# High parts of weight sums one step later, and blocks decoded one quad later, in an attention and two-layer kernel

## Chip, cores and metric

One core of a Trainium2 chip. The metric is the device time of one execution in microseconds (us), as the median of several runs.

## What is computed

```python
def reference(**kwargs):
    attn_out = _attn_ref(**attn_kwargs)        # chunked linear attention with decay, (4, 8, 768, 32)
    x = attn_out.transpose(0, 2, 1, 3).reshape(B * S, H * D)          # 3072 tokens x 256
    x = _moe_ref(x=x, **moe_kwargs)            # h = max(x @ w_in, 0);  (h * h) @ w_out
    return _moe2_ref(x=x, **moe2_kwargs)       # h = x @ w_in; (h * clip(h + 3, 0, 6) / 6) @ w_out
```

Both layers have 256 inputs and outputs and 2048 inner columns; all values are float32.

## The kernel before

**Tiles.** The 3072 tokens make six tiles of 512 columns, 0 to 5. The inner columns make 16 blocks of 128, or eight pairs of them, `q`. Every float32 operand is held as two numbers, a high part (ScalarE's rounding to the matmul's type) and a low part (the remainder, by VectorE or GpSimd), and each product is three matmuls: high by high, low by high, high by low.

**Stages.** Attention and the first layer of tiles 0 to 3 run together in 64 steps, numbered 0 to 63 (`ORDER`); a step is one tile and one inner block, with six matmuls into `h` (L582) and six into `y` (L616). After the matmuls of a step, ScalarE writes `ga` (the relu), VectorE squares it (L595; in some early steps ScalarE), ScalarE makes its high part `gha` (L597), and VectorE its low part `gla` (L599); the `y` matmuls of a step come two steps later. Steps 48 to 63 are tile 3; `ga3_5` is tile 3, inner block 5, step 53.

From there on the tiles are worked in pairs, by 32 *quads*, numbered 0 to 31: quads 0 to 7 are the first layer of tiles 4 and 5 (`a`), quads 8 to 15, 16 to 23 and 24 to 31 the second layer of three pairs of tiles (`b`, 0 to 2). A quad is one `q`: two inner blocks by two tiles. Its four products into the inner layer are made with seven, by sums and differences of the operands: weight sums in slots 0 to 10 of a block (4 to 6 are the sums that a product needs beside the weights), and operands `b11`, `b21`, `b22`, `t1` to `t4`, each with sum, high and low. Products are named p1 to p7, and collect in three PSUM banks, X, V and Z (L732): X p1, V p2, X p6, X p7, Z p5, X p4, Z p3. ScalarE copies X out as `s1`, `u2` and `u3` (L737) before the next product adds to it, and VectorE adds (L741) to get the four results `c11`, `c22`, `c12`, `c21`; c22 is taken from Z before p3 adds to Z. Then come the nonlinearity (L749 to L766), high parts `ghc` (L772), low parts `glc` (L775), and six matmuls into `y` for each (L788).

**Weight blocks.** The first layer's weights are already split for steps 0 to 63. For its quads the sums are needed too: `Weights.renew(q)` adds high and low (`whole`, VectorE, L507) and makes four sums (`sums`, GpSimd, L500); `Weights.both(q)` then makes high parts (`high`, ScalarE, L537: tiles `ea`, three slots, and `ah`, one slot) and low parts (`lower`, GpSimd, L544). The second layer's blocks `j` (0 to 15, two for each `q`) come from memory as they are decoded: `early` (E, ScalarE, L477), `begin` (B, VectorE, two operations `lowb`, L481 and L486), `end` (M: VectorE's merge into `wtb`, L491; GpSimd's sums for even `j`; the load of block `j` + 2), then high and low of the first slots and of the sums (F, G: `part`) or of all (H: `both`).

**What sets the order.** The schedule is written out by hand: each engine runs what is emitted, in that order, and waits by semaphores. `at(g, point, f)` hangs a job on a place: `g` below 64 is a step, where the jobs run after `gha` is issued and before `gla`; 1000 + g is quad g with points 0, 1, 6, 2, 3, 5, 4 in the order of `emit`. For the second layer's blocks a table of strings, one for each quad, gives point, letter and block: `5M10` is `end(10)` at point 5. For the operands, rows give the distance in quads from the first quad that uses them, the point, `s`, `h`, `l` or `L` (sum, high, low by VectorE, low by GpSimd), and the operand:

```python
    for q in range(NQ - 2):
        at(52 + 2 * q, 0, lambda q=q: w1.renew(q))
        at(53 + 2 * q, 0, lambda q=q: w1.both(2 * q))
```

Here NQ is 8: blocks 0 to 5 take steps 52 to 63, blocks 6 and 7 quads 0 and 1.

Of the kernel before, what the change touches and what calls it, by code (L numbers as in the profile page):

```python
# [41 lines left out]
NQ = DFF // (2 * P)  # L42
# [36 lines left out]
def attn_mlp_mlp(ctx: ExitStack, tc, a, bT, cT, bK, x, w1i, w1o, w2i, w2o, yT):  # L79
# [352 lines left out]
    class Weights:  # L432
# [21 lines left out]
        def at(self, q, k, i, n=1):  # L454

            if (self.pre, q) in own:
                return own[self.pre, q][k][:, i:i + n]
            if 4 <= i < 7:
                return self.ext[q][:, i - 4 + 3 * (k == "l"):][:, 0:n]
            d = self.hi if k == "h" else self.lo  # L460
            return d[q][:, i - 3 * (i > 6):][:, 0:n]
# [432 lines left out]
    w1 = w["a"] = Weights(w1i, w1o, "a")  # L894
# [122 lines left out]


    for q in range(NQ - 2):
        at(52 + 2 * q, 0, lambda q=q: w1.renew(q))  # L1020
        at(53 + 2 * q, 0, lambda q=q: w1.both(2 * q))
    for q in range(NQ - 2, NQ):
        at(1000 + q - 6, 5, lambda q=q: w1.renew(q))
        at(1001 + q - 6, 1, lambda q=q: w1.both(2 * q))
# [8 lines left out]
             "G": lambda j: w2.part(j, 1)}  # L1033
    for g, plan in enumerate(("6E2 2B2 5M2", "2E3 2B3 5M3", "2E4 2B4 5M4", "1F2 1G2 6H3 2E5 2B5 5M5",
# [3 lines left out]
        for d in plan.split():  # L1038
            at(1000 + g, int(d[0]), lambda f=does2[d[1]], j=int(d[2:]): f(j))
# [9 lines left out]
    def operands(g, key, plan):  # L1049
        for dg, p, f, n in plan:  # L1050
            if f == "s" and key == ("b", NPAIR - 1):
                at(g + dg, p, lambda n=n: later(key, n))
                continue
            at(g + dg, p, lambda f={"s": oper_sum, "h": oper_high, "l": oper_low, "L": by_pool}[f], n=n: f(key, n))
# [6 lines left out]
    operands(1000 + NQ, ("b", 0),  # L1061
# [4 lines left out]
    for p in range(1, NPAIR):  # L1066
        operands(1000 + NQ * (p + 1), ("b", p),
# [4 lines left out]

    def ready_second(t, f):
        run(16 * t + f, 1)
# [53 lines left out]
```

## Time and profile before

| | |
|---|---|
| median of 3 runs | 575.94 us (575.22 to 578.52) |
| profiled execution | 578.32 us, span of its instructions 576.5 us |
| mean granted TensorE clock | 0.988 of full speed |
| TensorE busy | 554.5 us, 96% of the span, 4110 matmuls |
| VectorE busy | 434.8 us, 75%, 669 instructions |
| ScalarE busy | 382.7 us, 66%, 692 instructions |
| GpSimd busy | 194.2 us, 34%, 260 instructions |
| chain that ended last, by engine | TensorE 85%, VectorE 7%, issue 3%, ScalarE 2%, GpSimd 2%, DMA 1% |

PE is TensorE, DVE VectorE, ACT ScalarE, POOL GpSimd. Times in the profile count from the start of the span. Line numbers (L537) are those of the kernel before; buffer numbers are left out of tile names, so `ea` in a row stands for `ea0` to `ea7`, and the number in a name such as `wta3s` is the block. The chain follows the last instruction back, at each step to what released it; "issue" is time in which an engine waited for nothing that the profile shows. An engine that waits for nothing starts its next instruction before the one ahead is shown as ended, so starts are nearer to each other than durations say.

### The profile page before, as it was taken

The page shows a single profiled execution, that of the slowest core. Times are in us where ns is not written, and L with a number is a line of the kernel's source. Part 1 is how long each engine was busy: PE and PEld are TensorE (multiplying, and loading weights), DVE is VectorE, ACT ScalarE, POOL GpSimd, SP SyncE. Part 2 cuts the span into 40 slices and gives each one's busy share as a digit, 9 for nine tenths or more (in the row PEclk, how much of TensorE's full clock was granted, in tenths as well). Part 3 has the DMA queues.
Part 4 walks back from the last instruction along what each step waited for, and adds up shares of the span by engine and source line. Part 5 has one row for each costly group of instructions (what it writes and reads, how often), then busy time and mean ns, then how long its engine had stood idle before and what let it go on. Part 6 is the DMA issues. An engine that isn't in the chain of part 4 may idle for free.

```text
span 576.5 us, 10490 instructions
## 1 busy us (share of the span) xinstructions
PE 554.5 (96%) x4110; PEld 442.3 (77%) x4110; DVE 434.8 (75%) x669; ACT 382.7 (66%) x692; POOL 194.2 (34%) x260
## 2 busy tenths in 40 slices
PE   7689999999999999799998999999999999999996
PEld 4457777778787877588886788888888888888884
DVE  8687777666555766698899998998967788776774
ACT  5576877455444655677787777787766678676663
POOL 3464443320000877476876632740000600000000
PEclk9789999999999999899999999999999999999999
DMA  7895453213000100111221111000200000200002
GB/s 209 204 253 158 121 148 111 74 49 101 2 1 26 49 0 2 35 40 36 74 74 36 55 56 38 0 2 0 74 0 1 1 2 1 74 0 1 0 2 73
DMA packets 26481, 31.43 MB, mean 55 GB/s; under 512 B 2144, under 2 KB 21056, under 8 KB 26432
## 3 DMA queue, kind: packets, MB, share of 16 engines
q1 hardware_dynamic: 24528, 29.85, 18.4%
q10 hardware_dynamic: 1904, 0.92, 0.6%
q8 instruction: 32, 0.52, 0.4%
q14 instruction: 17, 0.14, 0.1%
HBM read 27.41 MB, written 3.35 MB: 53 GB/s over the span
## 4 chain that ended last, share of the span: by engine, by line
PE 85%; DVE 7%; issue 3%; ACT 2%; POOL 2%; DMA 1%; SPq 0%; ACTq 0%; DVEq 0%; POOLq 0%
PE y L788 27%; PE ya L616 14%; PE X L732 14%; PE ha L582 14%; PE Z L732 7%; PE V L732 3%; PE att L363 2%; DVE glc L775 2%; DVE c L741 1%; PE att L350 1%; PE att L331 1%; PE big L890 1%; DVE c L764 1%; DMA xb<-in_x 1%; PE att L377 1%
## 5 line engine op out<-in xcount | busy, mean ns | idle before, releaser
L775 DVE TENSOR_TENSOR glc<-c,ghc 128x512 fp32r<-128x512 f32 x128 | 96.4, 759 | 8.1 <-ACT ghc L772 7.1
L772 ACT ACTIVATE ghc<-c 128x512 fp32r<-128x512 f32 x128 | 77.7, 629 | 2.4 <-DVE c L766 1.9
L788 PE MATMUL y<-glc,bh 128*128 128x512 f32 x192 | 74.9, 390 | 0.0
L788 PE MATMUL y<-ghc,bh 128*128 128x512 f32 x192 | 74.8, 390 | 0.0
L788 PE MATMUL y<-ghc,bl 128*128 128x512 f32 x192 | 74.7, 389 | 0.0
L766 DVE SCALAR_TENSOR_TENSOR c<-rc,c 128x512 f32<-128x512 f32 x72 | 52.7, 731 | 22.0 <-ACT rc L752 22.0
L752 ACT ACTIVATE rc<-c,three 128x512 f32<-128x512 f32 x72 | 52.0, 722 | 25.0 <-DVE c L741 24.9
L599 DVE TENSOR_TENSOR gla<-ga,gha 128x512 fp32r<-128x512 f32 x64 | 48.9, 764 | 24.1 <-ACT gha L597 23.3
L597 ACT ACTIVATE gha<-ga 128x512 fp32r<-128x512 f32 x64 | 40.6, 635 | 36.0 <-DVE ga L595 35.7
L595 DVE TENSOR_TENSOR ga<-ga,ha 128x512 f32<-128x512 f32 x48 | 32.9, 686 | 38.9 <-ACT ga L589 38.8
L741 DVE TENSOR_TENSOR c<-Z,u 128x512 f32<-128x512 f32 x64 | 43.9, 686 | 21.0 <-PE Z L732 20.4
L589 ACT ACTIVATE ga<-ha 128x512 f32<-128x512 f32 x64 | 37.8, 590 | 30.9 <-PE ha L582 30.9
L737 ACT COPY u<-X 128x512 f32<-128x512 f32 x64 | 37.6, 587 | 27.4 <-PE X L732 27.1
L616 PE MATMUL ya<-gha,ah 128*128 128x512 f32 x128 | 53.0, 414 | 0.2
L582 PE MATMUL ha<-act_h,ah 128*128 128x512 f32 x128 | 51.1, 401 | 2.3 <-ACT ah L522 2.3
L582 PE MATMUL ha<-act_h,al 128*128 128x512 f32 x128 | 51.1, 401 | 0.3 <-POOL al L524 0.2
L616 PE MATMUL ya<-gla,ah 128*128 128x512 f32 x128 | 50.7, 396 | 0.0
L616 PE MATMUL ya<-gha,al 128*128 128x512 f32 x128 | 50.7, 396 | 0.0
L582 PE MATMUL ha<-act_l,ah 128*128 128x512 f32 x128 | 50.6, 397 | 0.0
L544 POOL TENSOR_TENSOR bl<-wtb,bh 128x256 fp32r<-128x256 f32 (+1 forms) x34 | 30.5, 922 | 35.8 <-ACT bh L537 29.3
L788 PEld LDWEIGHTS y<-glc,bh 128*128 128x128 f32 x192 | 36.0, 188 | 8.4 <-DVE glc L775 0.9
L788 PEld LDWEIGHTS y<-ghc,bh 128*128 128x128 f32 x192 | 36.0, 188 | 7.7 <-ACT ghc L772 0.4
(295 smaller groups left out, 1247.1 us busy)
## 6 DMA issues: line engine op xcount, KB each, us to landing
rawa<-in_w1i SPq DMA_DIRECT2D x8, 512.0 KB
rawa<-in_w1o SPq DMA_DIRECT2D x8, 512.0 KB
rawb<-in_w2i SPq DMA_DIRECT2D x8, 512.0 KB
rawb<-in_w2o SPq DMA_DIRECT2D x8, 512.0 KB
xb<-in_x SPq DMA_DIRECT2D x24, 128.0 KB
ef<-scr SPq DMA_DIRECT2D x10, 256.0 KB
out_yT<-xf SPq DMA_DIRECT2D x10, 256.0 KB
bc<-in_cT SPq DMA_DIRECT2D x6, 256.0 KB
```

What stands on the lines that cost most here:

```text
L582: nc.tensor.matmul(out=h, lhsT=wt[fb][:, k, fo * P:fo * P + P], rhs=xt[t][:, k, :], start=i == 0, stop=i == 5)
L589: nc.scalar.activation(out=g, in_=h, func=AF.Relu)
L597: nc.scalar.activation(out=gh, in_=g, func=AF.Copy)
L599: nc.vector.tensor_tensor(out=gl, in0=g, in1=gh.bitcast(F32), op=ALU.subtract)
L616: nc.tensor.matmul(out=ys[m], lhsT=terms[i][0][fb][:, fo, m * P:m * P + P], rhs=terms[i][1], start=first and i == 0, stop=last and i == 2)
L732: nc.tensor.matmul(out=self.ps[bank], lhsT=lhsT, rhs=rhs, start=start and i == 0, stop=stop and i == 2, skip_group_check=True)
L741: nc.vector.tensor_tensor(out=self.sb[c], in0=self.ps[bank], in1=self.sb[n], op=ALU.add)
L752: nc.scalar.activation(out=self.sb["r" + c], in_=src, func=AF.Relu, bias=three)
L766: nc.vector.scalar_tensor_tensor(out=self.sb[c], in0=self.sb["r" + c], scalar=6.0, in1=src, op0=ALU.min, op1=ALU.mult)
L772: nc.scalar.activation(out=self.gh[c], in_=self.sb[c], func=AF.Copy)
L775: nc.vector.tensor_tensor(out=self.gl[c], in0=self.sb[c], in1=self.gh[c].bitcast(F32), op=ALU.subtract)
L788: nc.tensor.matmul(out=ys[t][m], rhs=terms[i][1], lhsT=w[self.pre].at(self.q, terms[i][0], 7 + 2 * (1 - f) + m)[:, 0], start=first and i = ...
```

## The change

Three things move. The high and low parts of blocks 0 to 4 of the first layer (`both`) go from one step after their sums to two, ahead of the next block's `renew`; those of block 5 go from step 63 to point 1 of quad 0. In the table of the second layer's blocks, block 10's B and M go to later points of quad 7, and all that concerned blocks 11 to 15 goes one quad later, F10 and G10 staying in quad 8. And in the operands' rows a few highs and lows move: the low of t3 of the first pair from point 5 to point 2 of quad 7; for the later pairs the highs of b11, b21 and t2 by a point or a few, and for pair 1 the low of t2 goes from VectorE to GpSimd.

```diff
--- before.py
+++ after.py
@@ -1017,8 +1017,10 @@
 
 
     for q in range(NQ - 2):
+        if q:
+            at(52 + 2 * q, 0, lambda q=q: w1.both(2 * q - 2))
         at(52 + 2 * q, 0, lambda q=q: w1.renew(q))
-        at(53 + 2 * q, 0, lambda q=q: w1.both(2 * q))
+    at(1000, 1, lambda: w1.both(2 * (NQ - 3)))
     for q in range(NQ - 2, NQ):
         at(1000 + q - 6, 5, lambda q=q: w1.renew(q))
         at(1001 + q - 6, 1, lambda q=q: w1.both(2 * q))
@@ -1033,7 +1035,7 @@
              "G": lambda j: w2.part(j, 1)}
     for g, plan in enumerate(("6E2 2B2 5M2", "2E3 2B3 5M3", "2E4 2B4 5M4", "1F2 1G2 6H3 2E5 2B5 5M5",
                               "1F4 1G4 6H5 2E6 2B6 5M6", "1E7 1B7 2M7 2E8 6F6 5B8 5M8 4G6", "1H7 6E9 2B9 2F8 5M9 4G8",
-                              "1H9 6E10 2B10 5M10", "6E11 2B11 2F10 5M11 5G10", "6E12 2B12 2H11 5M12",
+                              "1H9 6E10 5B10 4M10", "2F10 5G10", "6E11 2B11 5M11", "2H11 6E12 2B12 5M12",
                               "6E13 2B13 2F12 5M13 5G12", "6E14 2B14 2H13 5M14", "6E15 2B15 2F14 5M15 5G14", "2H15")):
         for d in plan.split():
             at(1000 + g, int(d[0]), lambda f=does2[d[1]], j=int(d[2:]): f(j))
@@ -1061,14 +1063,14 @@
     operands(1000 + NQ, ("b", 0),
              ((-4, 0, "s", "t1"), (-4, 2, "s", "t2"), (-4, 4, "h", "b11"), (-3, 1, "h", "b21"), (-3, 2, "s", "t4"),
               (-2, 0, "s", "t3"), (-2, 1, "h", "t2"), (-2, 1, "l", "b11"), (-2, 5, "l", "b21"), (-1, 1, "l", "t2"),
-              (-1, 1, "h", "t3"), (-1, 2, "h", "t1"), (-1, 2, "L", "t1"), (-1, 5, "l", "t3"), (-1, 4, "h", "t4"),
+              (-1, 1, "h", "t3"), (-1, 2, "h", "t1"), (-1, 2, "l", "t3"), (-1, 2, "L", "t1"), (-1, 4, "h", "t4"),
               (-1, 4, "L", "t4"), (0, 1, "h", "b22"), (0, 1, "L", "b22")))
     for p in range(1, NPAIR):
         operands(1000 + NQ * (p + 1), ("b", p),
-                 ((-4, 0, "s", "t1"), (-4, 2, "s", "t2"), (-3, 0, "s", "t4"), (-3, 2, "s", "t3"), (-3, 6, "h", "b11"),
-                  (-3, 5, "h", "b21"), (-2, 1, "l", "b11"), (-2, 6, "h", "t2"), (-2, 2, "l", "b21"), (-2, 5, "l", "t2"),
-                  (-1, 1, "h", "t3"), (-1, 2, "l", "t3"), (-1, 6, "h", "t1"), (-1, 5, "l", "t1"), (-1, 2, "h", "t4"),
-                  (0, 1, "l", "t4"), (-1, 5, "h", "b22"), (0, 2, "l", "b22")))
+                 ((-4, 0, "s", "t1"), (-4, 2, "s", "t2"), (-3, 0, "s", "t4"), (-3, 2, "s", "t3"), (-3, 1, "h", "b11"),
+                  (-2, 6, "h", "b21"), (-2, 1, "l", "b11"), (-2, 5, "h", "t2"), (-2, 2, "l", "b21"),
+                  (-2, 5, "L" if p == 1 else "l", "t2"), (-1, 1, "h", "t3"), (-1, 2, "l", "t3"), (-1, 6, "h", "t1"),
+                  (-1, 5, "l", "t1"), (-1, 2, "h", "t4"), (0, 1, "l", "t4"), (-1, 5, "h", "b22"), (0, 2, "l", "b22")))
 
     def ready_second(t, f):
         run(16 * t + f, 1)
```

ScalarE, steps 53 to 56, before (each name ends in a number of its own; `oa2b21` is an operand's high part):

```order
L597 ACTIVATE gha3_5_2745<-ga3_5_2747 128x512
L537 ACTIVATE ea0_2729<-wta0s_2728 128x384
L537 ACTIVATE ah0_342<-wta0s_2728 128x128
L589 ACTIVATE ga3_6_2773<-ha3_6_2764 128x512
L597 ACTIVATE gha3_6_2771<-ga3_6_2773 128x512
L685 ACTIVATE oa2b21_2790<-xin4_1965 128x512
L589 ACTIVATE ga3_7_2802<-ha3_7_2793 128x512
L597 ACTIVATE gha3_7_2800<-ga3_7_2802 128x512
L537 ACTIVATE ea1_2784<-wta1s_2783 128x384
L537 ACTIVATE ah1_430<-wta1s_2783 128x128
```

and now:

```order
L597 ACTIVATE gha3_5_2745<-ga3_5_2747 128x512
L589 ACTIVATE ga3_6_2768<-ha3_6_2759 128x512
L597 ACTIVATE gha3_6_2766<-ga3_6_2768 128x512
L537 ACTIVATE ea0_2729<-wta0s_2728 128x384
L537 ACTIVATE ah0_342<-wta0s_2728 128x128
L685 ACTIVATE oa2b21_2790<-xin4_1965 128x512
L589 ACTIVATE ga3_7_2802<-ha3_7_2793 128x512
L597 ACTIVATE gha3_7_2800<-ga3_7_2802 128x512
L589 ACTIVATE ga3_8_2823<-ha3_8_2814 128x512
L597 ACTIVATE gha3_8_2821<-ga3_8_2823 128x512
L537 ACTIVATE ea1_2784<-wta1s_2783 128x384
L537 ACTIVATE ah1_430<-wta1s_2783 128x128
```

`ea0` and `ah0` stand behind the `gha` of step 54 instead of step 53, and `ea1`, `ah1` behind that of step 56; blocks 2 to 4 likewise. On VectorE and GpSimd no row of these steps moves.

ScalarE, the end of step 63 and the start of quad 0, before:

```order
L597 ACTIVATE gha3_15_3020<-ga3_15_3022 128x512
L537 ACTIVATE ea5_3004<-wta5s_3003 128x384
L537 ACTIVATE ah5_1146<-wta5s_3003 128x128
L737 COPY s10_3043<-X0_3039 128x512
L685 ACTIVATE oa2b22_3058<-xin5_2366 128x512
L737 COPY u20_3063<-X0_3039 128x512
L772 ACTIVATE ghc11_0_3065<-c11_0_3049 128x512
```

and now:

```order
L597 ACTIVATE gha3_15_3020<-ga3_15_3022 128x512
L737 COPY s10_3038<-X0_3034 128x512
L537 ACTIVATE ea5_3004<-wta5s_3003 128x384
L537 ACTIVATE ah5_1146<-wta5s_3003 128x128
L685 ACTIVATE oa2b22_3058<-xin5_2366 128x512
L737 COPY u20_3063<-X0_3034 128x512
L772 ACTIVATE ghc11_0_3065<-c11_0_3044 128x512
```

The copy `s1` of quad 0 (printed `s10`, block X0) now stands ahead of `ea5` and `ah5`; the high of b22, `u2` and the rest stay behind them.

VectorE in quad 8, from the copy of the first layer's last output, before (`lowb` is the decoding, the row into `wtb` the merge):

```order
L800 COPY xf4_3935<-y0_01_3127 128x512
L481 TENSOR_SCALAR lowb11_3946<-rawb11_3754 128x512
L486 TENSOR_SCALAR lowb11_3946<-rawb11_3754 128x512
L741 TENSOR_TENSOR c22_8_3959<-Z8_3955,u38_3944 128x512
L800 COPY xf5_3964<-y0_11_3151 128x512
L766 SCALAR_TENSOR_TENSOR c22_8_3959<-rc22_8_3973,c22_8_3959 128x512
L491 SCALAR_TENSOR_TENSOR wtb5_3820<-wtb5_3820,lowb11_3946 128x512
L741 TENSOR_TENSOR c12_8_3987<-Z8_3955,u28_3924 128x512
```

and now:

```order
L800 COPY xf4_3934<-y0_01_3127 128x512
L741 TENSOR_TENSOR c22_8_3955<-Z8_3951,u38_3943 128x512
L800 COPY xf5_3960<-y0_11_3151 128x512
L766 SCALAR_TENSOR_TENSOR c22_8_3955<-rc22_8_3969,c22_8_3955 128x512
L741 TENSOR_TENSOR c12_8_3980<-Z8_3951,u28_3924 128x512
L775 TENSOR_TENSOR glc22_8_3983<-c22_8_3955,ghc22_8_3982 128x512
```

The decoding and the merge of block 11 are gone from this quad, and the addition for c22 follows the copy. In quad 7 the low of t3 now stands ahead of the addition of c22, the decoding of block 10 behind it, and its merge behind the low of c22.

## Rows read from the trace of the kernel before

**Rows 1.** Busy time of four stretches: us of length, then per engine busy us (instructions).
```profile
212.00:244.90 32.90, 29.66 (x112) 21.05 (x111) 21.63 (x33) 19.71 (x40) 20.40 (x33) 0.95 0.05 15
238.00:242.00 4.00, 3.97 (x11) 3.13 (x12) 3.35 (x6) 2.67 (x6) 0.89 (x3) 0.57 0.01 2
...
303.50:336.50 33.00, 30.05 (x128) 23.30 (x128) 31.41 (x43) 24.44 (x46) 20.58 (x23) 1.00 0.16 48
336.50:565.00 228.50, 228.50 (x1009) 189.03 (x1008) 180.63 (x277) 163.12 (x275) 34.18 (x42) 1.00 0.05 15
```

**Rows 2.** Chain of waits, 212 to 240: start us, us, what.
```profile
222.57 0.98 POOL wta3s L500
223.56 0.07 issue
...
224.46 0.02 ACT ea L537
```

**Rows 3.** Timeline of ScalarE: start us, us, instruction, [idle before <-releaser].
```profile
206.01 0.53 ACT L537 ACTIVATE ea<-wta0s 128x384 fp32r<-128x384 f32 x1 [2.24 <-POOL wta0s L500]
...
220.27 0.63 ACT L597 ACTIVATE gha<-ga 128x512 fp32r<-128x512 f32 x1 [0.76 <-DVE ga L595]
...
236.74 0.52 ACT L537 ACTIVATE ea<-wta5s 128x384 fp32r<-128x384 f32 x1 [1.15 <-POOL wta5s L500]
...
237.36 0.57 ACT L737 COPY s<-X 128x512 f32<-128x512 f32 x1
...
239.47 0.59 ACT L737 COPY u<-X 128x512 f32<-128x512 f32 x1 [1.01 <-PE X L732]
...
242.65 0.59 ACT L737 COPY u<-X 128x512 f32<-128x512 f32 x1
```

**Rows 4.** Timeline of VectorE, steps 58 and 59.
```profile
220.16 0.88 DVE L507 TENSOR_TENSOR wta3s<-ah,al 128x512 f32<-128x512 f32 x1
220.96 0.68 DVE L599 TENSOR_TENSOR gla<-ga,gha 128x512 fp32r<-128x512 f32 x1
...
222.55 0.68 DVE L691 TENSOR_TENSOR oa2t<-xin,oa2t 128x512 fp32r<-128x512 f32 x1
223.33 0.77 DVE L599 TENSOR_TENSOR gla<-ga,gha 128x512 fp32r<-128x512 f32 x1
```

**Rows 5.** Timeline of GpSimd, low parts of block 3.
```profile
225.06 1.16 POOL L544 TENSOR_TENSOR ea<-wta3s,ea 128x256 fp32r<-128x256 f32 x2 [0.64 <-ACT ea L537]
226.18 0.46 POOL L544 TENSOR_TENSOR al<-wta3s,ah 128x128 fp32r<-128x128 f32 x1
```

**Rows 6.** Timeline of TensorE: X of quad 0; Z of quads 6, 7, 8.
```profile
238.03 0.56 PE L732 MATMUL X<-oa2t,ea 128*128 128x512 f32 x1 [2.85 <-issue]
...
307.54 0.50 PE L732 MATMUL Z<-oa2b,ea 128*128 128x512 f32 x1 [1.59 <-DVE c L741]
...
318.22 0.50 PE L732 MATMUL Z<-oa2b,ea 128*128 128x512 f32 x1 [0.19 <-DVE c L741]
...
329.89 0.50 PE L732 MATMUL Z<-ob0b,bh 128*128 128x512 f32 x1 [1.15 <-DVE c L741]
```

**Rows 7.** Timeline of VectorE, quads 7 and 8.
```profile
316.14 0.41 DVE L481 TENSOR_SCALAR lowb<-rawb 128x512 uint32<-128x512 uint32 x1
...
317.50 0.67 DVE L741 TENSOR_TENSOR c<-Z,u 128x512 f32<-128x512 f32 x1
...
320.53 0.80 DVE L775 TENSOR_TENSOR glc<-c,ghc 128x512 fp32r<-128x512 f32 x1 [0.56 <-ACT ghc L772]
...
327.36 1.00 DVE L481 TENSOR_SCALAR lowb<-rawb 128x512 uint32<-128x512 uint32 x1
...
329.16 0.67 DVE L741 TENSOR_TENSOR c<-Z,u 128x512 f32<-128x512 f32 x1
```

**Rows 8.** Timeline of GpSimd, quads 7 and 8.
```profile
318.84 2.80 POOL L500 TENSOR_TENSOR wtb<-wtb 128x128 f32<-128x128 f32 x4 [0.67 <-DVE wtb L491]
...
324.28 2.01 POOL L691 TENSOR_TENSOR ob0b<-xf,ob0b 128x256 fp32r<-128x256 f32 x2 [0.28 <-ACT ob0b L685]
```

## Prediction

> **What bounds the kernel now.** I read the busy time of four stretches first [rows 1]. Between 336.50 and 565.00 TensorE has 1009 matmuls of 512 columns, one of them begun earlier: 1008 starts in 228.50 us, one each 0.227 us without a gap. There TensorE bounds the kernel, and that is its pace. Between 212.00 and 244.90 there are 111 starts in 32.90 us; at pace they take 25.2, so 7.7 us are lost. Between 303.50 and 336.50 it is 127 starts in 33.00, 28.8 at pace, 4.2 lost. The change works in these two stretches, so 11.9 us is all that it can win.
>
> Then I read the chain of waits of the first stretch [rows 2] and the engines beside it [rows 3 to 5]. It is a ring of three engines, one turn for each weight block: ScalarE's high parts (L537, `ea`, `ah`) stand in its queue until GpSimd's sums (L500) are done; the next step's `ga` stands behind them, VectorE's `whole` (L507) behind that, and the next sums behind `whole`. `ea0` starts at 206.01 and `ea5` at 236.74 [rows 3]: 6.15 us a turn. TensorE's work for two steps is 24 matmuls, 5.44 us. Each turn takes 0.7 us off TensorE's lead, then off its time. At the end comes the dearest piece: quad 0's copy `s1` stands behind `ea5` and `ah5` and starts only at 237.36 [rows 3], and TensorE, whose X p6 overwrites that bank, idles 2.85 us up to 238.03 [rows 6]. After that idle the granted clock is 0.57 from 238 to 242 [rows 1], mostly the lower level, 1.2 GHz.
>
> In the second stretch three matmuls named Z wait for VectorE's addition of c22, in quads 6, 7 and 8: idle 1.59, 0.19 and 1.15 us [rows 6], each with some 0.26 more until matmuls are back at 0.227. That is 1.85, 0.45 and 1.4; the rest of the 4.2 is small gaps in quads 6 and 9. VectorE is busy 31.41 of the 33.00 us [rows 1], and in quads 7 and 8 the decoding of a block stands ahead of that addition [rows 7].
>
> **The change part by part.**
>
> High parts one step later, steps 54 to 63. Only ScalarE's queue changes; VectorE's and GpSimd's rows keep their order. `ea` no longer stops the step whose `whole` the sums need, so the old ring opens. A smaller one is left, on GpSimd: `ea`, low parts, the next sums, the next `ea`. Its turn: the low parts end at 226.64, 2.18 us after `ea3` began at 224.46 [rows 2, 5]; four sums, each 0.46 if nothing disturbs it, as the low part of the same size [rows 5], with 0.07 between two [rows 2], make 2.1 more: 4.35 in all. VectorE does disturb them: the sum at 222.57 took 0.98 [rows 2] while the low of an operand (222.55) and a `gla` (223.33) ran [rows 4]. So a hit costs 0.25 to 0.5. Two steps hold four such VectorE operations. I place them against `ea` at T, with TensorE at its pace: from `gha` at 220.27 [rows 3] the `gla` follows 0.69 later, the next step's low 2.28, its `gla` 3.06, and `whole` stands 0.11 ahead of `gha` [rows 4]. Now `ea` and `ah` (0.63) stand between `gha` and the next step, and `ea` begins 0.54 after `gha`. So `gla` is at T+0.15, where GpSimd is waiting for `ea`; low and `gla` at T+2.4 and T+3.15 hit the sums; the next `whole` comes at T+4.8. Two hits: the sums end at T+4.85 to T+5.35, and `ea` is due at T+5.44. The ring keeps TensorE's pace, if narrowly, and these steps lose nothing.
>
> The Trainium skill, SBUF — State Buffer, section SBUF: two separate sides, says that VectorE with two SBUF inputs and GpSimd hold their shared port in turn, each for its whole instruction, and that the loser fully blocks. Here the held-up sum ended at 223.55; by that rule it could only begin when the low ended at 223.23 and would end at 223.70, so the trace shows slightly less. By the rule a turn would be up to 7.1 us, and the change could lose.
>
> The turn into quad 0. At pace, `y` of c11 would begin at 212.0 + 25.2 = 237.2 instead of 244.9; X p7 stands 12 matmuls ahead of it, 234.5, and X p4 six ahead, 235.8. `ea0` stays at 206.0, since sums 0 do not move; four turns of 5.44 later is `ea4`, 227.8; sums 5 end 4.9 to 5.35 after it, so `ea5` starts at 232.7 to 233.1. `s1` now stands ahead of it and the 2.85 idle at X p6 goes. What is late next is `u2`, which X p7 waits for: behind `ea5` and `ah5` (0.62) and the high of b22 (0.52) it ends some 1.7 after `ea5` began, 234.4 to 234.8. X p7 loses 0 to 0.4. Then `u3`: before, 6.50 us lie from the start of `ea5` to the end of `u3`, of which 1.01 are idle before `u2` [rows 3], 0.47 go to `s1`, and 0.7, an estimate, to shorter waits and to overlap lost at each. Without these it is 4.3. `u3` ends at 237.0 to 237.4, and X p4 starts up to 1.6 late. With 0.3 until the matmuls are dense again I keep a loss of 1.9, idle in two pieces. Idle of 1.59 before a Z left the clock at 1.00 [rows 1, 6], so I count no half-speed matmuls. First stretch: 7.7 - 1.9 = **5.8 us won**.
>
> Quad 7. VectorE's c22 now comes behind the low of t3 (0.68 us like the low in [rows 4], the next starting 0.6 after it) and not behind the decoding that begins at 316.14. It starts at 316.74 instead of 317.50 [rows 7]; were the low held up by GpSimd by 0.5, at 317.3. The 0.45 go, or half of it. Quad 8. The decoding that begins at 327.36 leaves the quad, c22 (329.16) comes up to 1.8 us earlier [rows 7], and the 1.4 go. Quad 9's small gap goes with VectorE's backlog, 0.2. Quad 6's 1.85 stays, since nothing that moves stands ahead of it. Together 2.0.
>
> What the moved merge of block 10 delays: GpSimd's sums for it began at 318.84, and its lows of t4 and b22 stand behind them until 326.29 [rows 8], 7.2 us without the idle. The merge now stands behind the low of c22, which waits for ScalarE (320.53 [rows 7], 0.45 earlier now) and takes 0.6, the merge 0.7: the sums start near 321.4 and b22's low ends near 328.6. Quad 8's Z p3 (329.89 [rows 6], less 0.45 and 1.4) wants it for its third matmul at 328.5. No gain here, a loss between 0 and 1; I take 0.2, as the margin is nil. Second stretch: **1.8 us won**.
>
> Blocks 11 to 15 a quad later, and operands of later pairs. Every quad from 9 on carries one block's decoding as quads 9 to 12 did before, and each consumer has at least a quad left. The loads that `5M` issues (512 KB each) move with their consumers; SP's queue keeps its order. The fullest queue is ScalarE's in quad 13, with four extra operations (`E15`, two highs of block 14, the high of b11); quad 15 of before has four operand highs as well and lies in the stretch at full pace [rows 1]. One low of t2 goes from VectorE to GpSimd, which is busy 34 of those 228 us. I cost all of it at nothing; without that cover one such quad could cost 1.85, as quad 6 does. TensorE's and SP's queues do not change.
>
> Sum: 5.8 + 1.8 = 7.6 us. The profiled execution took 578.32 and would take 570.7; its gaps should be those of the median run, 575.94, which gives **568.3 us**.
>
> **The rivals.** (a) The ring on GpSimd does not open: all VectorE operations hit it and it stays at 6.15. Then `ea5` comes at 236.8; 4.3 for ScalarE, 0.1, six matmuls and 0.3 put `y` of c11 at 242.8, 2.1 won, with the lower clock again. With the second stretch 572.0. For it: the turn computed above leaves only 0.1 to 0.6 us. Against it: one hit fewer is enough.
> (b) GpSimd's queue in quads 7 and 8 takes back what VectorE gives: b22's low ends 2 us later than computed and Z p3 waits for it. The second stretch gives nothing: 570.3. For it: no margin; against it: GpSimd idles 0.28 between those lows [rows 8].
> (c) Slower: all four VectorE operations of a turn hold GpSimd up for their whole length, 0.69 to 0.88 [rows 4]. The turn is then at least 4.35 + 4 x 0.7 = 7.15, `ea5` comes at 241.8, and `y` of c11 at 247.8, 2.9 later than now; 577.0 with the 1.8 won elsewhere, and up to 579 if ten more matmuls run at the lower clock. It decides from a turn of 6.9 us on. Against it: the trace's hits cost 0.5 at most, and the `gla` beside `ea` meets no sum. This is the case that the rule of the Trainium skill above would make.
>
> **How the numbers follow.** The measurement tells 0.5%, 2.9 us, from no change; faster means below 573.1. Forecast 0.66, all of it faster. (a) 0.18, two thirds faster, the rest within 0.5%. (b) 0.10, faster. (c) 0.06, half of it slower by over 0.5%. Faster 0.88, same 0.09, slower 0.03. The range goes down to both stretches without any loss that moved (7.7 + 2.1: 566.1) and up past (b) to (a), 572.2; what is left out is (c) and the tails.
>
> **What would show it.** Right: `ea0` to `ea4` 5.4 to 5.5 us apart and started by ScalarE's own order, with no wait for L500; no gap in TensorE before quad 0; there two idles below 1.7 before X p7 and X p4, and the clock at 1.00; Z of quads 7 and 8 with next to no idle, quad 6's still near 1.6. Wrong: `ea` waiting for L500 in each turn and turns of 6 us or more (a, c), a Z in quad 8 that waits for GpSimd (b), or new gaps of TensorE after quad 12.

## The result, and the profile after

| | before | after |
|---|---|---|
| median, range, runs | 576.18 us (575.22 to 578.52), 5 | 570.3 us (569.7 to 571.76), 5 |
| ratio, 95% interval | | 0.9895 [0.9867, 0.9923] |
| profiled execution, span | 578.32, 576.5 us | 569.82, 568.1 us |
| mean granted clock | 0.988 | 0.993 |
| busy TensorE, VectorE, ScalarE, GpSimd | 554.5, 434.8, 382.7, 194.2 us | 550.0, 434.5, 382.1, 194.2 us |

The change is faster, by 5.9 us in the medians; 568.3 was forecast, with 566.1 to 572.2 as the range. This profiled execution of after was 0.7 us earlier than that of before when step 52 began, ahead of every edit, so an instruction that stands 7 us earlier after quad 0 has won 6.3 of them.

The same four stretches after the change, cut so that the same matmuls fall into the first, third and last (112, 128 and 1009 on TensorE, as in [rows 1]); behind them quads 13 and 14, from TensorE's first matmul of each quad to that of the next. Columns: stretch, length, busy TensorE, weight loads, VectorE, ScalarE, GpSimd (instructions), clock, DMA share, GB/s:

```profile
211.27:237.86 26.59, 25.71 (x112) 20.60 (x111) 21.34 (x31) 17.89 (x38) 18.89 (x32) 1.00 0.03 5
235.00:239.00 4.00, 3.12 (x13) 2.12 (x13) 3.59 (x7) 3.21 (x7) 1.24 (x2) 1.00 0.38 122
296.50:327.30 30.80, 29.19 (x128) 23.64 (x127) 29.33 (x41) 24.60 (x45) 20.45 (x23) 1.00 0.11 35
327.30:556.70 229.40, 229.27 (x1009) 188.68 (x1008) 181.26 (x278) 162.91 (x275) 36.15 (x44) 1.00 0.06 17
363.90:374.30 10.40, 10.40 (x46) 8.21 (x45) 9.58 (x14) 8.31 (x15) 8.45 (x11) 1.00 0.01 2
374.30:385.20 10.90, 10.77 (x46) 8.28 (x45) 9.67 (x16) 8.59 (x16) 5.00 (x7) 1.00 0.00 1
```

Quads 13 and 14 of the kernel before, to compare:

```profile
373.20:383.50 10.30, 10.30 (x46) 8.37 (x45) 9.08 (x13) 8.67 (x15) 7.49 (x9) 1.00 0.01 2
383.50:393.70 10.20, 10.20 (x46) 8.45 (x45) 9.21 (x15) 7.24 (x13) 0.18 (x1) 1.00 0.00 1
```

Against [rows 1] the first stretch takes 26.59 us and not 32.90, 6.3 less. The granted clock beside quad 0's idle is 1.00, where 0.57 stood. The second stretch takes 30.80 and not 33.00, 2.2 less. But the last one takes 229.40 where the same 1009 matmuls took 228.50: **0.9 us came back in a stretch that ran at full pace before.**

ScalarE after, start us, us, instruction, idle before and its releaser; it answers to [rows 3]:

```profile
205.66 0.53 ACT L537 ACTIVATE ea<-wta0s 128x384 fp32r<-128x384 f32 x1 [0.29 <-POOL wta0s L500]
...
210.84 0.51 ACT L537 ACTIVATE ea<-wta1s 128x384 fp32r<-128x384 f32 x1
...
216.15 0.51 ACT L537 ACTIVATE ea<-wta2s 128x384 fp32r<-128x384 f32 x1
...
221.59 0.51 ACT L537 ACTIVATE ea<-wta3s 128x384 fp32r<-128x384 f32 x1
...
227.03 0.51 ACT L537 ACTIVATE ea<-wta4s 128x384 fp32r<-128x384 f32 x1
...
230.04 0.57 ACT L737 COPY s<-X 128x512 f32<-128x512 f32 x1
232.03 0.53 ACT L537 ACTIVATE ea<-wta5s 128x384 fp32r<-128x384 f32 x1 [1.42 <-POOL wta5s L500]
...
233.18 0.56 ACT L737 COPY u<-X 128x512 f32<-128x512 f32 x1
...
235.68 0.60 ACT L737 COPY u<-X 128x512 f32<-128x512 f32 x1
```

The high parts start 5.18, 5.31, 5.44 and 5.44 us apart; none from `ea1` to `ea4` waits for GpSimd's sums (L500). `s1` (230.04) is done before `ea5`, which does wait, 1.42 us. `u2` ends at 233.74 and `u3` at 236.28.

GpSimd after, in the last turn and in quads 7 and 8 (it answers to [rows 5, 8]):

```profile
227.62 1.26 POOL L544 TENSOR_TENSOR ea<-wta4s,ea 128x256 fp32r<-128x256 f32 x2 [1.06 <-ACT ea L537]
...
229.26 2.74 POOL L500 TENSOR_TENSOR wta5s<-wta5s 128x128 f32<-128x128 f32 x4
...
314.07 3.13 POOL L500 TENSOR_TENSOR wtb<-wtb 128x128 f32<-128x128 f32 x4 [2.81 <-DVE wtb L491]
317.17 2.33 POOL L691 TENSOR_TENSOR ob0t<-fb0t,ob0t 128x256 fp32r<-128x256 f32 x2
319.46 1.44 POOL L691 TENSOR_TENSOR ob0b<-xf,ob0b 128x256 fp32r<-128x256 f32 x2
```

Four sums take 2.74 us and end at 232.00, 4.97 after `ea4` began.

TensorE after: the largest gap of quad 0, Z of quad 6, and two of the new gaps (the `y` of quad 13, which TensorE runs at the start of quad 14); it answers to [rows 6]:

```profile
236.34 0.50 PE L732 MATMUL X<-oa2t,ah 128*128 128x512 f32 x1 [0.88 <-ACT u L737]
...
300.46 0.96 PE L732 MATMUL Z<-oa2b,ea 128*128 128x512 f32 x3 [1.61 <-DVE c L741]
...
376.37 0.50 PE L788 MATMUL y<-glc,bh 128*128 128x512 f32 x1
...
378.77 0.50 PE L788 MATMUL y<-glc,bh 128*128 128x512 f32 x1
```

X p6 stands in its place now; X p4 waits 0.88 for `u3`; quad 6's Z waits as before. Quads 7 and 8 have no idle before Z. The two rows of `y` show no idle, but a `glc` operand came late: the matmul ahead of each started 0.45 and 0.46 us earlier, and not 0.227.

VectorE after, in quad 7, quad 8 and quad 13 (it answers to [rows 7]):

```profile
309.05 0.68 DVE L691 TENSOR_TENSOR ob0t<-xf,ob0t 128x512 fp32r<-128x512 f32 x1
309.65 0.68 DVE L741 TENSOR_TENSOR c<-Z,u 128x512 f32<-128x512 f32 x1
...
319.42 0.68 DVE L741 TENSOR_TENSOR c<-Z,u 128x512 f32<-128x512 f32 x1
...
367.70 1.17 DVE L766 SCALAR_TENSOR_TENSOR c<-rc,c 128x512 f32<-128x512 f32 x1
...
372.91 1.06 DVE L766 SCALAR_TENSOR_TENSOR c<-rc,c 128x512 f32<-128x512 f32 x1 [0.79 <-ACT rc L752]
373.89 1.23 DVE L491 SCALAR_TENSOR_TENSOR wtb<-wtb,lowb 128x512 uint32<-128x512 uint32 x1
```

c22 follows the low of t3 by 0.60 in quad 7 and stands at 319.42 in quad 8. The last three rows stand ahead of the new gaps: operations that take 0.68 us elsewhere took 1.17, 1.06 and 1.23 (the merge of block 15) while GpSimd made sums for the operands of pair 1. VectorE was then the chain's longest part from 365 to 382. That the 0.9 comes from these sums is tried below.

### The profile page after: what moved, and what is told of

It is laid out like the page before. It is cut to its first block, busy times and chain, and to the rows that moved or that the text cites. A ratio compares the mean times of both kernels' runs of the same rounds, so it can differ in the third digit from the quotient of the medians.

```text
span 568.1 us, 10494 instructions
## 1 busy us (share of the span) xinstructions
PE 550.0 (97%) x4110; PEld 441.9 (78%) x4110; DVE 434.5 (76%) x668; ACT 382.1 (67%) x692; POOL 194.2 (34%) x262
## 4 chain that ended last, share of the span: by engine, by line
PE 73%; DVE 8%; POOL 8%; ACT 4%; issue 3%; DMA 3%; SPq 1%; ACTq 0%; POOLq 0%; DVEq 0%
PE y L788 26%; PE X L732 13%; PE ya L616 10%; PE ha L582 10%; PE Z L732 6%; PE V L732 3%; DVE glc L775 2%; DMA ef<-scr 2%; DVE c L741 1%; PE att L363 1%; POOL ea L544 1%; DVE wtb L491 1%; DVE c L766 1%; PE att L331 1%; POOL bc L295 1%
## 5 line engine op out<-in xcount | busy, mean ns | idle before, releaser
L544 POOL TENSOR_TENSOR bl<-wtb,bh 128x256 fp32r<-128x256 f32 (+1 forms) x34 | 30.9, 933 | 43.5 <-ACT bh L537 43.5
```

## Where TensorE loses time, run by run

For this table I took every distance between the starts of two 512-column matmuls over 0.257 us, less 0.227, and added them up: in the first 58 us after the 301st matmul into `h`, from there to the end of quad 9, and later. Losses of the profiled execution, us:

| | 301st `h` starts | first stretch | quads 0 to 9 | later | all |
|---|---|---|---|---|---|
| before | 191.62 | 7.64 | 4.17 | 0.32 | 12.1 |
| after | 190.88 | 1.39 | 2.05 | 1.19 | 4.6 |
| a1_change_again | 191.22 | 1.39 | 2.05 | 1.15 | 4.6 |
| e1_high_parts_only | 190.14 | 1.37 | 3.64 | 0.31 | 5.3 |
| e2_tables_only | 190.66 | 7.57 | 2.01 | 1.09 | 10.7 |
| e3_block5_after_u3 | 191.98 | 1.48 | 1.99 | 1.06 | 4.5 |
| e4_block9_after_c22 | 191.85 | 1.39 | 2.08 | 1.07 | 4.5 |
| e5_both | 190.92 | 1.50 | 1.99 | 1.11 | 4.6 |
| e6_two_more_hits | 193.36 | 6.79 | 2.02 | 1.11 | 9.9 |
| e7_psum_in_place | 190.75 | 3.96 | 2.01 | 1.14 | 7.1 |
| e8_old_operand_rows | 190.54 | 1.39 | 2.01 | 0.84 | 4.2 |
| e9_sums_in_quad_9 | 191.54 | 1.38 | 3.49 | 0.25 | 5.1 |
| e10_sums_spread | 191.14 | 1.39 | 2.35 | 0.25 | 4.0 |
| e11_spread_old_rows | 190.09 | 1.37 | 2.02 | 0.26 | 3.7 |

In every run the last matmul starts at the first column plus the last plus 367.2 to 367.7 us, so these two columns are all but 0.5 us of what differs between the profiled executions. The first column moves by up to 3.3 us between executions, with the same code ahead of it in all; in the runs looked at (before, after, e1, e6, e11) the difference is there by step 10, and from there to step 50 each takes 129.8 us; some 0.25 in "later" lie at the kernel's end in all.

## The experiments

**The change once more.** No edit.

> The changed kernel again, beside the runs below on one chip. If TensorE's gaps tell the whole difference (11.9 lost before, 4.4 after), it is 7.5 us off, ratio 0.987. If the first comparison's 5.9 us is the truth, ratio 0.990.

569.86 us, ratio 0.9875 [0.9857, 0.9894]. The losses are those of the first profile of the change, to 0.04 us. The medians give 5.9 and 6.8 us, the gaps 7.5.

**The two halves, each alone.** e1 is the kernel before with the first part of the diff (high and low parts a step later, block 5 in quad 0); e2 is the change with that part undone:

```diff
     for q in range(NQ - 2):
-        if q:
-            at(52 + 2 * q, 0, lambda q=q: w1.both(2 * q - 2))
         at(52 + 2 * q, 0, lambda q=q: w1.renew(q))
-    at(1000, 1, lambda: w1.both(2 * (NQ - 3)))
+        at(53 + 2 * q, 0, lambda q=q: w1.both(2 * q))
```

> The kernel before with the first edit alone (high parts a step later, block 5 in quad 0). Theory: the two stretches are won separately. The first loses about 1.4 us of TensorE instead of 7.7, the Z waits of quads 6, 7 and 8 stay at 1.6, 0.2 and 1.2 us: 6.3 us off, ratio 0.989. Rival, that the second stretch only repeats lateness from the first: the Z waits shrink too, 8 us off.

> The kernel before with the other edits alone (blocks 10 to 15 and the operands' rows). Theory: turns of the ring stay at 6.15 us and quad 0 idles 2.8 us before X p6; quads 7 and 8 lose their 0.45 and 1.4, quads 12 to 14 add 1.0 in small gaps as in the changed kernel: 1 us off, ratio 0.998, not to be told from no change by the time alone. Rival, that these edits bring the most: 4 us off or more.

e1: 570.56 us, ratio 0.9891 [0.9858, 0.9923]. e2: 576.09 us, 0.9979 [0.9961, 0.9996]. By the table the first part takes 6.3 us out of the first stretch. Quads 0 to 9 lose 3.64 and not 4.17, which the theory did not have: quad 8's Z idles 0.59, where 1.15 stood. TensorE and VectorE of e1 there:

```profile
321.43 0.50 PE L732 MATMUL Z<-ob0b,bh 128*128 128x512 f32 x1 [0.59 <-DVE c L741]
```

```profile
319.49 0.41 DVE L481 TENSOR_SCALAR lowb<-rawb 128x512 uint32<-128x512 uint32 x1
```

The first `lowb` takes 0.41 here and 1.00 in [rows 7], with the same code in this quad. In both traces a GpSimd operation (`bl`, L544) starts 0.02 to 0.03 us ahead of it; before, `lowb` ends 0.28 after the end of that one, in e1 it is that one which ends 0.59 after `lowb`. Which of two nearly equal starts goes first is worth half a microsecond. The tables take 1.6 to 2.2 out of quads 0 to 9 and put 0.8 to 0.9 into later ones. TensorE of e2 in quad 0, and the clock beside it:

```profile
237.02 1.18 PE L732 MATMUL X<-oa2t,ea 128*128 128x512 f32 x3 [2.84 <-issue]
```

```profile
237.00:241.00 4.00, 3.98 (x11) 3.17 (x12) 3.50 (x6) 2.81 (x6) 0.90 (x3) 0.57 0.01 2
```

The idle of before is there again, and with it the clock of 0.57, mostly the level of 1.2 GHz.

**Quad 0: block 5 behind `u3`.** What is left of the first stretch is X p4's wait for `u3`, behind `ea5`. e3 lets `ea5` follow `u3`:

```diff
-    at(1000, 1, lambda: w1.both(2 * (NQ - 3)))
+    at(1000, 2, lambda: w1.both(2 * (NQ - 3)))
```

> The changed kernel with block 5's high parts at point 2 of quad 0, behind u3, instead of point 1. Theory (u2 and u3 stand behind ea5, which waits 1.4 us for the sums): the 1.4 us that TensorE loses in quad 0 go, to 0.2 or less, and nothing comes back: 1.2 us faster than the changed kernel. Rival (the loss is c22's chain, or goes to the relu of c22 behind ea5): the gap moves to Z p3 and the time stays within 0.3 us.

570.13 us, ratio 0.9886 [0.9869, 0.9903]: no gain. TensorE's X p4, then VectorE's next `whole`:

```profile
236.83 0.50 PE L732 MATMUL X<-oa2t,ah 128*128 128x512 f32 x1 [0.49 <-ACT u L737]
```

```profile
238.89 0.69 DVE L507 TENSOR_TENSOR wta6s<-ah,al 128x512 f32<-128x512 f32 x1 [1.39 <-POOL al L544]
```

The gap before X p4 falls by 0.4 only: `u2` no longer stands behind `ea5` but waits 1.43 us for TensorE, and from `u2` to `u3` ScalarE's queue takes 2.5 us without idle, as in the change. And `whole` of block 6 waits 1.39 us for block 5's low parts; TensorE's new gaps come in quad 1, the largest of them before a Z at 248.51, 0.27 late. The lateness moved.

**Quad 6: block 9 behind c22.** The same treatment that the change gives quads 7 and 8:

```diff
-"1H7 6E9 2B9 2F8 5M9 4G8"
+"1H7 6E9 5B9 2F8 4M9 4G8"
```

> The changed kernel with block 9's decoding at point 5 and its merge at point 4 of quad 6, behind the addition of c22, as the change did for block 10 in quad 7. Theory (the decoding ahead of c22 makes the 1.77 us idle of Z in quad 6): idle 0 to 0.3, 1.6 us faster than the changed kernel. Rival (VectorE is full from quad 5 on, so the lateness only moves): the gap comes back in quad 7 or 8, within 0.5 us.

570.04 us, ratio 0.9883 [0.9866, 0.99]: no gain. TensorE in quads 6 and 7:

```profile
306.44 0.50 PE L788 MATMUL y<-glc,ah 128*128 128x512 f32 x1 [0.59 <-DVE glc L775]
...
311.69 0.96 PE L732 MATMUL Z<-oa2b,ea 128*128 128x512 f32 x3 [0.49 <-DVE c L741]
```

Quad 6's Z no longer waits, a `y` 7 us later waits for `glc`, and then quad 7's Z; quads 0 to 9 lose 2.08 us, and 2.05 without the edit. VectorE is busy 10.33 of 10.50 us (286 to 296.5) and then 16.22 of 16.50, what GpSimd holds it up included. This move finds no room there; that no other could is not shown.

**Both together.** e5 has both edits.

> Both of these moves on the changed kernel. If each gap goes by itself: 2.8 us faster than the changed kernel, some 10 us or 1.8% faster than before. If they come back elsewhere: less than 1 us faster than the changed kernel.

570.23 us, ratio 0.9883 [0.9862, 0.9904]. Neither edit helps the other.

**The price of VectorE beside GpSimd.** From step 52 on each `gla` is made twice (e6, both operands in SBUF); in e7 the added one takes `in1=h` from PSUM, and the second overwrites it:

```diff
+        if ORDER.index((t, f)) >= 52:
+            nc.vector.tensor_tensor(out=gl, in0=g, in1=gh.bitcast(F32), op=ALU.subtract)
```

> The changed kernel with the low part gla of each step from 52 on computed twice by VectorE, so that a turn has two more operations with two operands in SBUF. Theory (GpSimd is held up by such operations, 0.25 to 0.5 us each): the sums of a block take 3.0 to 3.8 us instead of 2.74, a turn of ea is 5.4 to 5.9 us and ScalarE waits for the sums again; 0.5 to 2.5 us slower than the changed kernel. Rival (GpSimd's own pace sets it): the sums stay at 2.74 us and the time moves by less than 0.5 us.

> The changed kernel with one more VectorE operation per step from 52 on, as in the run with two more hits, but with one operand in PSUM instead of SBUF (its result is overwritten). VectorE works as long as there. Theory (only two operands in SBUF hold GpSimd up): sums at 2.7 to 2.8 us, no wait of ea for them, time within 0.5 us of the changed kernel. Rival (VectorE's own lateness is what delays): as slow as the run with two more hits.

e6: 575.14 us, ratio 0.9961 [0.994, 0.9983]. e7: 572.07 us, 0.9902 [0.987, 0.9934]. Both are slower than was expected, e6 by some 5 us against the change and not 0.5 to 2.5, e7 by some 2 and not at most 0.5. First e6, ScalarE and GpSimd, then e7, the same:

```profile
222.03 0.51 ACT L537 ACTIVATE ea<-wta2s 128x384 fp32r<-128x384 f32 x1
...
228.21 0.51 ACT L537 ACTIVATE ea<-wta3s 128x384 fp32r<-128x384 f32 x1
```

```profile
222.61 1.71 POOL L544 TENSOR_TENSOR ea<-wta2s,ea 128x256 fp32r<-128x256 f32 x2 [0.90 <-PE ha L582]
...
224.71 3.19 POOL L500 TENSOR_TENSOR wta3s<-wta3s 128x128 f32<-128x128 f32 x4
```

```profile
217.78 0.51 ACT L537 ACTIVATE ea<-wta2s 128x384 fp32r<-128x384 f32 x1
...
223.53 0.51 ACT L537 ACTIVATE ea<-wta3s 128x384 fp32r<-128x384 f32 x1
```

```profile
218.37 1.61 POOL L544 TENSOR_TENSOR ea<-wta2s,ea 128x256 fp32r<-128x256 f32 x2 [0.89 <-ACT ea L537]
...
220.37 2.86 POOL L500 TENSOR_TENSOR wta3s<-wta3s 128x128 f32<-128x128 f32 x4
```

A turn takes 6.18 and 5.75 us, but `ea` does not wait for the sums. In both runs VectorE's instructions follow one another without idle through two steps, and their starts add up to the turn: VectorE's own time became the bound, which of the four cases only e7's rival had. GpSimd's part can still be read, operation by operation. First the kernel before: VectorE's `ga`, whose operand `ha` is in PSUM, and a sum that GpSimd begins beside it; then e7: the old `gla` (L601 in e7's own numbering), both operands in SBUF, and a sum beside it:

```profile
221.94 0.69 DVE L595 TENSOR_TENSOR ga<-ga,ha 128x512 f32<-128x512 f32 x1 [0.30 <-ACT ga L589]
```

```profile
222.04 0.46 POOL L500 TENSOR_TENSOR wta3s<-wta3s 128x128 f32<-128x128 f32 x1
```

```profile
221.65 0.71 DVE L601 TENSOR_TENSOR gla<-ga,gha 128x512 fp32r<-128x512 f32 x1
```

```profile
221.89 0.79 POOL L500 TENSOR_TENSOR wta3s<-wta3s 128x128 f32<-128x128 f32 x1
```

Beside the operand in PSUM the sum takes 0.46, as when nothing runs beside it. Beside two operands in SBUF it takes 0.79 and ends 0.32 after VectorE's operation. [rows 2, 4] say the same: the low ends at 223.23, the sum beside it at 223.55. It holds in all the traces from 200 us on: of 624 GpSimd operations on 128x128 that took over 0.52 us, 622 end 0.30 to 0.34 after a VectorE operation beside them, and the 174 that had only VectorE operations with an operand in PSUM beside them took 0.45 to 0.47. The other way, 905 of 909 held-up VectorE operations (128x512, both operands in SBUF) end 0.53 to 0.57 after a GpSimd operation. So each side waits for the end of the other's operation, and loses what was left of that when it came, less some 0.14 (0.79 - 0.46 = 0.33, where 0.47 of the `gla` were left).

The sums end 4.97 us after `ea` in the change, 5.87 in e6 and 5.45 in e7. In e6 two more of GpSimd's operations are held in a turn, 0.45 each. In e7 it is one more, though the added operation holds none: it pushes the old `gla` onto a low part (the longer of the two `ea` rows, 0.91 in place of 0.46). 5.87 is 0.43 over TensorE's 5.44; whether GpSimd would have closed the ring with VectorE free is not shown.

**The new gaps: rows or sums.** e8 puts the later pairs' operand rows back as they were. e9 moves GpSimd's sums for pair 1 to where it idles, e10 spreads them with the device that the last pair already uses (`later`: a copy of one column out of a quad's `s1` holds them back), and e11 is e10 with the rows of e8. The new places hold for pair 1 alone, and the rows are written here as they read for it:

```diff
e9
-                 ((-4, 0, "s", "t1"), (-4, 2, "s", "t2"), (-3, 0, "s", "t4"), (-3, 2, "s", "t3"), ...
+                 ((-7, 0, "s", "t1"), (-7, 2, "s", "t2"), (-7, 5, "s", "t4"), (-6, 0, "s", "t3"), ...
e10
-            if f == "s" and key == ("b", NPAIR - 1):
+            if f == "s" and key[0] == "b" and key[1] > 0:
-                 ((-4, 0, "s", "t1"), (-4, 2, "s", "t2"), (-3, 0, "s", "t4"), (-3, 2, "s", "t3"), ...
+                 ((-7, 2, "s", "t1"), (-6, 2, "s", "t2"), (-5, 2, "s", "t4"), (-4, 2, "s", "t3"), ...
```

> The change with the operand rows of the later pairs as they were before (highs of b11, b21 and t2 at their old points, pair 1's low of t2 back on VectorE). It asks where the four new gaps of TensorE in quads 12 and 13 come from, 0.9 us in all in the profile of the change (0.18 and less in that of before). Theory: from the table, which puts the decoding and merging of blocks 13 and 14, and GpSimd's sums for block 14, beside GpSimd's sums of pair 1's operands; VectorE's operations are then held up in both quads. The rows have no part in it: the gaps in front of y stay at 0.7 to 1.2 us and the time within 0.5 us of 570.1. Rival: the rows, by their highs on ScalarE and lows on VectorE at other points, make the gaps: under 0.3 us are left of them, and the time is 569.4.

> The change with GpSimd's four pairs of sums for pair 1's operands (1.9 us each) taken from quads 12 and 13 to quad 9 and the start of quad 10, where GpSimd has nothing to do for 15.7 us. Theory: VectorE is held up in quads 12 and 13 by these sums, its merge there takes 1.23 us instead of 0.68 and two multiplications 1.17 and 1.06; with the sums gone these take 0.7 to 0.9, the gaps of TensorE in quads 12 and 13 fall from 0.9 to under 0.3, none as large comes in quads 9 and 10, where VectorE has 1.6 us to spare in each quad, and the time is 569.2 to 569.6. Rival 1: the hold-ups move along with the sums, and gaps of 0.5 to 1 us come in quads 9 and 10: no gain, 570.1. Rival 2: the gaps in quads 12 and 13 come from elsewhere (VectorE's own work, or ScalarE's highs) and stay at 0.7 or more.

> The change with GpSimd's sums for pair 1's operands spread over four quads, one pair of sums (1.9 us) in each of quads 9 to 12, held to its quad by a copy of one column out of that quad's s1 as the last pair's already are. Packed into quad 9 they took the gaps of quads 12 and 13 away but made one of 1.4 us in front of Z in quad 9. Theory: what costs is how many of GpSimd's operations stand beside one quad of VectorE, which has 1.0 to 1.6 us to spare in each; one pair of sums holds VectorE up by 0.5 to 0.8 us, so spread they fit: gaps from quad 9 to quad 13 sum to under 0.2 us, and the time is 0.7 to 0.9 us below the change's: 569.2 to 569.5, a ratio of 0.986 to 0.988. Rival: the hold-ups only move again, gaps of 0.5 us and more come in quads 10 to 12: 570.

> The spread sums together with the operand rows of the later pairs as they were before the change. Of the gaps in quads 12 and 13 the old rows left 0.56 of 0.93 us. Theory: with the sums spread VectorE has time in both quads and the rows decide nothing: the gaps and the time of the spread sums with the change's rows, within 0.3 us. Rival: the rows are worth 0.4 us by themselves, and this one is the faster of the two by that.

e8: 569.46 us, ratio 0.9867 [0.9838, 0.9896]. The gaps at the `y` of quads 12 and 13 are 0.56 and not 0.93: between the two expectations, so in this execution the rows have a part in it, of 0.4. (By the table in the code quads 12 and 13 carry the decoding of blocks 14 and 15, not of 13 and 14.)

e9: 570.59 us, 0.9889 [0.9862, 0.9917]. The gaps at the `y` of quads 12 and 13 are gone to the last one, and Z of quad 9 waits instead. GpSimd, VectorE and TensorE there:

```profile
324.90 1.89 POOL L674 TENSOR_TENSOR fb1t<-xf,xf 128x256 f32<-128x256 f32 x2
326.75 4.67 POOL L674 TENSOR_TENSOR fb1t<-xf,fb1t 128x256 f32<-128x256 f32 x4
331.38 1.78 POOL L674 TENSOR_TENSOR xf<-xf 128x256 f32<-128x256 f32 x2
```

```profile
328.46 2.37 DVE L775 TENSOR_TENSOR glc<-c,ghc 128x512 fp32r<-128x512 f32 x2
330.75 0.95 DVE L481 TENSOR_SCALAR lowb<-rawb 128x512 uint32<-128x512 uint32 x1
331.74 0.87 DVE L486 TENSOR_SCALAR lowb<-rawb 128x512 uint16<-128x512 uint16 x1
```

```profile
333.24 0.96 PE L732 MATMUL Z<-ob0b,eb 128*128 128x512 f32 x3 [1.17 <-DVE c L741]
```

GpSimd waits for nothing and runs all four sums in one piece, whatever quad they are written in. Beside them VectorE's decoding takes 0.95 and 0.87 us, and a pair of `glc` 2.37; in [rows 7] the first of the two `lowb` took 0.41 once, and 1.00 where GpSimd was at work. The theory was right on the cause, rival 1 on the time.

e10: 569.29 us, 0.9866 [0.9845, 0.9888]. e11: 568.11 us, 0.9857 [0.9837, 0.9876]. From quad 9 to the `y` of quad 13 neither has a gap; e11's last stretch, beside the 229.40 of the change:

```profile
326.00:554.50 228.50, 228.50 (x1009) 189.33 (x1009) 180.10 (x280) 163.19 (x276) 35.38 (x44) 1.00 0.06 17
```

That is the 228.50 of [rows 1] again. So the cause of the new gaps is shown: GpSimd's sums for pair 1 in quads 12 and 13, beside the blocks' work as the table now places it (the decoding of block 15 in quad 13, for one). Before, the same sums stood there under the old table; in e9 to e11 the new table stands without them in quad 13; neither has the gaps. Which of the moved blocks it takes was not tried. The rows decide nothing in TensorE's gaps once the sums are spread: the profiled executions of e10 and e11 lie 1.5 us apart, of which 1.05 stand in the table's first column and 0.35 in one gap in quad 5, which the edits don't touch. The medians lie 1.2 apart, where 0 to 0.4 was expected, with ranges that overlap; why stays open. e11 is the fastest kernel measured here, 1.0 us below the change in the gaps; its interval overlaps that of the change.

## Why the prediction was right, and where it wasn't

**High parts one step later: right, with its sizes.** The ring opened, `ea` 5.4 us apart, and GpSimd's turn, computed as 4.85 to 5.35 us to the end of the sums, measured 4.97. The two hits took 2.74 - 2.1 = 0.64 together, 0.3 each. (2.18 and 2.1 make 4.28 and not 4.35, which moves nothing; and the 0.98 that it counted as one hit or two is one: that sum ends 0.32 after the low, and it is the next sum that ends 0.32 after the `gla`.) `ea5` came 5.00 after `ea4` (4.9 to 5.35 forecast), `s1` ahead of it, `u2` as forecast, `u3` at the early end. The loss left was taken as 1.9 and measured 1.39, since X p4 lost 1.05 and not up to 1.6 and X p7 0.19. 6.25 us were won, 5.8 forecast. Block 5's place and the high parts' place were not tried apart.

**The clock: right.** It stayed at 1.00 beside idles of 0.88 and 1.61, and e2 shows 0.57 again behind 2.84.

**Second stretch: right, the 0.2 for GpSimd's queue was not needed.** Its sums began at 314.07; the forecast's 321.4, less 7.0 for what lies ahead, is 314.4. b22's low ended 320.90, and Z p3 did not wait. 2.1 to 2.2 won, 1.8 forecast; against e1 it is 1.6. Half a microsecond of this term is the one `lowb` that took 1.00 before and 0.41 in e1.

**Blocks 11 to 15 and the operands "at nothing": wrong, by 0.85 us.** The step that failed is the choice of the cover: I looked for the fullest queue, found ScalarE's in quad 13, and compared it with a quad of before that held as much. What came late was VectorE: busy 9.58 of 10.4 us in quad 13 and 9.67 of 10.9 in quad 14, where 9.08 of 10.3 and 9.21 of 10.2 stood. It got the decoding and the merge of block 15 in quad 13, and there they meet GpSimd's sums: GpSimd, whose 34 us over 228 were counted as light, is busy 8.45 us in quad 13 and 5.00 in quad 14. Its work in quad 13 is not new by itself (7.49 us before, and TensorE lost nothing); the two together are new. The text named new gaps after quad 12 as a sign against it; they came, at a price below the 1.85 of one full quad.

**From gaps to the median: the step that missed most.** By gaps 7.6 were forecast and 7.5 came, too much in one term and too little in another. But 568.3 rests on subtracting them from 575.94, the median of before, and the median came out at 570.3. "Its gaps should be those of the median run" was never shown: the executions without a profile have no gaps to read, and even e1's quads 0 to 9 lost 0.5 less than those of before, with the same code there. And three runs were few: the five groups of runs on record, on different chips, have medians of 576.2 to 577.7 for the kernel before, their 55 executions one of 577.0. Less 7.6 that is 569.4; the change's nine executions have 570.15, 6.8 less than before. So of the 2.0 missed some 1.0 is the low median of the first three runs, and some 0.8 is gaps that the median did not give back. The profiled execution took 569.82, where 570.7 was forecast for it; 0.7 of what it won lies ahead of step 52. How much of the 12.1 us the median execution of before lost stays open; 0.56 of it is the one `lowb`.

**The rivals.** (a) did not come: two hits of 0.3 leave 0.5 us of a turn. (b) did not come, though the median is its 570.3 to the tenth: that is luck (and 575.94 less 5.8 is 570.1). (c) did not come: two of the four operations of a turn met a sum, and each cost 0.3 and not its whole 0.69 to 0.88; in e6, with two more, 0.45 for each. The Trainium skill, SBUF — State Buffer, section SBUF: two separate sides, has the loser of the shared port blocked for the whole instruction, and the trace agrees: a held sum ends 0.32 after VectorE's operation. What (c) had wrong is the price it made of this rule: the wait is what is left of the other's operation, and 0.32 of a sum's 0.46 then follow, where the prediction added the whole 0.46 (223.70 for 223.55).

## What to carry to other kernels

Where an engine's queue carries a job that waits for another engine, put the job where its input is surely done: one step later, with block 5's move, opened a ring of three engines and won 6.3 of the 7.5 us. A job moved under "cover" has to be looked up on every engine of the quad it goes to, and with what runs beside it: average load did not show the collision here, and an engine that waits for nothing runs early and in one piece wherever its job is written, so that a small copy that waits is what spreads it. Where an engine has next to no spare time in a stretch, as VectorE in quads 5 and 6, a reordering can just move the gap (e4).

## What the hardware showed unexpectedly

- Overlap of VectorE and GpSimd costs both where VectorE has both operands in SBUF: the one that comes second ends a fixed time after the other's end, GpSimd's 128x128 sum 0.32 us (622 of 624 held ones), VectorE's 128x512 operation 0.55 (905 of 909). With a VectorE operand in PSUM the sum kept its 0.46 (222.04 of before, and 174 in all). An operation with a single tensor operand is no exception: the decoding took 0.95 beside GpSimd (e9) and 0.41 elsewhere.
- Of two starts 0.03 us apart, one order or the other was worth 0.56 us to TensorE (quad 8 of before and of e1).
- Idle of 2.85 and 2.84 us was followed by a granted clock of 0.57 over four microseconds; idle of 0.88 us (quad 0 after) by 1.00; the idle of 1.61 us in quad 6 left it there too.
- The same code ahead of step 52 took up to 3.3 us more or less from one execution to the next (190.09 to 193.36), more than the smaller half of this change is worth.
